# Reordering the first three tiles' layernorm, transposes and loads at the head of a fused attention and feed-forward kernel

## The chip, the cores and the metric

The kernel runs on one core of a Trainium2 chip. A core has TensorE (matrix products and transposes, PE in the profile, its weight loads PEld), VectorE (DVE), ScalarE (ACT), GpSimd (POOL) and SyncE (SP), which here issues every transfer. Each engine takes its own instructions in the order in which they were written; between engines they wait for one another through semaphores. The metric is the device time in microseconds. Three runs of the kernel before took 269.99, 270.53 and 270.79 us: median 270.53.

## The reference

x has 2048 tokens of width 640. It is normalised once, and the result goes through two branches, which are added to x:

```python
x = A_x
xn = _layernorm(x, axis=-1)
return x + _A_ref(xn, A_wqkv, A_w_phi, A_wo) + _B_ref(xn, B_w1, B_w3, B_w2)
```

Branch A is linear attention with 32 heads of width 20. q, k and v are slices of `xn @ wqkv`; q and k are multiplied by a small matrix per head, and phi is the softmax of that product beside the softmax of its negative:

```python
kv = jnp.einsum("bhsf,bhsd->bhfd", phi_k, v)
z  = jnp.einsum("bhsf->bhf", phi_k)
num = jnp.einsum("bhqf,bhfd->bhqd", phi_q, kv)
den = jnp.einsum("bhqf,bhf->bhq", phi_q, z)[..., None] + 1e-6
o = num / den        # heads joined again, then @ wo
```

Branch B is a gated feed-forward layer of width 1536: `(silu(xn @ w1) * (xn @ w3)) @ w2`. Everything comes in and goes out as bf16; products add up in float32.

## The kernel before

The tokens are cut into 16 tiles of 128, the width 640 into 5 chunks of 128. The order of the work is written out by hand (`manual_schedule`, line 127): what stands first in the text stands first on its engine's queue, and no planner moves it. The kernel has three stages: a head in which the tiles are normalised and transposed, V is formed and a few feed-forward products fill in (lines 617 to 702); a loop over tiles for k (706 to 717); and a loop over tiles for q, the attention's output and the result (721 to 751). The branch at line 754 isn't taken for these inputs. The change touches the head, and there tiles 0 to 3 above all.

**The steps of a tile.** `ln_stats` (209) has VectorE take statistics of each half of the tile's width (L213, 320 columns each) and join them (L216); a function given as `between` is called after the first half. `ln_root` (229) takes the square root on ScalarE (L232). `lx` (592) takes the reciprocal on VectorE (L594) and normalises the tile in place, there too (L267). For tiles 0 to 3 `x_transposed`, called `T`, makes five transposes on TensorE (L281) into one PSUM bank, and ScalarE copies them out in two parts, of 256 and of 384 columns (L285); `between` is called after the first. From tile 4 on the root is formed on POOL (`ln_pow`, `ln_newton`) and the transpose is a transfer (L277). `V` (602) runs `by_token` (295): per chunk two products, of 360 and 280 columns, ten in all, with xnT's chunk as the stationary operand and rows of the V weights `wv` as the moving one (L303). `between=(3, f)` calls f ahead of the fourth chunk's products. Three copies by ScalarE follow (L316).

**Loads.** SP's queue begins with x of tiles 0 and 1, three loads of `wv` and x of tiles 2 and 3 (146 to 151). Two more groups are held back: POOL writes one element into the destination from `ry`, the roots, and the load must follow that write. x of tiles 4 to 7 waits in this way for tile 0's root (L619), the first feed-forward weights for tile 1's (L624).

**Warm-up.** `warm(n)` issues n products of zeros on TensorE (L192), 48 ahead of everything and four between the transposes of tiles 0 and 1.

The order at the head, around the change:

```python
ln_stats(1)
ln_root(1)
...
lx(0, 1)
T(0)
warm(4)
lx(1, 1)
T(1)
ln_stats(2)
ln_root(2)
V(0)
```

So on ScalarE the queue is: root of tile 0, root of tile 1, two copies of tile 0, two of tile 1, root of tile 2, the copies of V of tile 0. Then follow tile 3's statistics with tile 2's normalise between the halves, V of tile 1 with tile 2's transposes ahead of its fourth chunk (and tile 3's root between tile 2's two copies), tile 3's normalise, and V of tile 2 with tile 3's transposes.

Of the kernel before, what the change touches and what calls it, by code (L numbers as in the profile page):

```python
# [12 lines left out]
def kernel(  # L13
# [30 lines left out]
    SAFE = 36.0  # L44
    BY_DMA = 4
    BY_ACT = (12, 13)
    WARM = 48


    NCH = 11  # L50
# [65 lines left out]
    def ld(dst, src):  # L116
        nc.sync.dma_start(out=dst, in_=src)
# [9 lines left out]
    with tc.manual_schedule():  # L127
        def ldT(dst, i, d):
            rows = slice(d * P, (d + 1) * P)
            nc.sync.dma_start_transpose(  # L130
                out=dst[:, :, rows], in_=A_wqkv[rows, i * D : (i + 1) * D]
            )
# [3 lines left out]
        def ld_tiles(t, n):  # L136
            ld(
                xin[:, (t // 4) % 3, t % 4 : t % 4 + n],
                x2[t * P : (t + n) * P, :].rearrange("(t p) d -> p t d", p=P),
            )  # L140

        def ld_wv(c, n):
            src = A_wqkv[c * P : (c + n) * P, 2 * D : 3 * D]
            ld(wv[:, c : c + n], src.rearrange("(c p) f -> p c f", p=P))
# [2 lines left out]
        ld_tiles(1, 1)  # L147
        ld_wv(0, 1)
        ld_wv(1, 2)
        ld_tiles(2, 2)  # L150
        ld_wv(3, 2)


        ident = one.tile([P, P], bf, name="ident")
# [35 lines left out]
        def warm(n):  # L190
            for _ in range(n):
                nc.tensor.matmul(idle[:, 0:P], nought[:], nought[:])  # L192

        warm(WARM)

# [13 lines left out]
        def ln_stats(t, between=None):  # L209
            xt = xin[:, (t // 4) % 3, t % 4, :]  # L210
            st = work.tile([P, 2, 6], f32, name="st")
            for i in range(2):
                nc.vector.bn_stats(out=st[:, i, :], in_=xt[:, i * HD : (i + 1) * HD])  # L213
                if i == 0 and between:
                    between()
            nc.vector.bn_aggr(out=mv[:, t, :], in_=st[:])  # L216
# [12 lines left out]
        def ln_root(t):  # L229

            r = slice(t, t + 1)
            nc.scalar.activation(  # L232
                out=ry[:, r], in_=mv[:, t, 1:2], func=AF.Sqrt, bias=eps[:, 0:1], scale=1.0
            )
# [24 lines left out]
        def ln_x(t):  # L259
            xt = xin[:, (t // 4) % 3, t % 4, :]  # L260
            if t in BY_ACT:
                nc.scalar.activation(
                    out=xt, in_=xt, func=AF.Identity,
                    scale=rstd[:, t : t + 1], bias=shift[:, t : t + 1],
                )
                return
            nc.vector.tensor_scalar(  # L267
                out=xt, in0=xt, scalar1=mv[:, t, 0:1], scalar2=rstd[:, t : t + 1],
                op0=ALU.subtract, op1=ALU.mult,
            )  # L270
# [21 lines left out]
        def tile_of(t):  # L292
            return slice(t * P, (t + 1) * P)
# [19 lines left out]
        def v_unit(dst, cols, between=(KD, None)):  # L313
            ps = by_token(cols, wv, "pv", CH, between)
            for p, c0, n, k in chunks(ps):
                nc.scalar.copy(  # L316
                    out=dst[:, c0 : c0 + n, 1 : 1 + k],
                    in_=p.rearrange("p (c e) -> p c e", c=n),
                )
# [272 lines left out]
        def lx(t0, n):  # L592
            if t0 < BY_DMA:
                nc.vector.reciprocal(out=rstd[:, t0 : t0 + n], in_=ry[:, t0 : t0 + n])  # L594
            for t in range(t0, t0 + n):
                ln_x(t)
# [3 lines left out]
        T = x_transposed  # L600

        def V(t, between=(KD, None)):
            v_unit(vaug[:, t], tile_of(t), between)
# [15 lines left out]
        nc.gpsimd.tensor_copy(out=xin[0:1, 1, 0, 0:1], in_=ry[0:1, 0:1])  # L619
        ld_tiles(4, 2)  # L620
        ld_tiles(6, 2)
        ln_stats(1)
        ln_root(1)
        nc.gpsimd.tensor_copy(out=w1[0:1, 0, 0:1], in_=ry[0:1, 1:2])  # L624
        ld_glu(0, 256)
# [1 line left out]
        ld_tiles(10, 2)  # L627
        ld_glu(256, 512)
        ld(wps[:], A_w_phi.rearrange("h j f -> (h j) f").rearrange("(c p) f -> p c f", p=P))
        lx(0, 1)  # L630
        T(0)
        warm(4)
        lx(1, 1)
        T(1)
        ln_stats(2)
        ln_root(2)
        V(0)

        def third():
            T(2, between=lambda: ln_root(3))  # L640
# [3 lines left out]
        lx(3, 1)  # L644
        V(2, between=(3, lambda: T(3)))
        nc.scalar.activation(out=table[:], in_=nought[:, 0:1], func=AF.Tanh)
        ld_tiles(12, 2)
        ld_tiles(14, 2)
        ldT(wkT, 1, 0)
        V(3)  # L650
        stats(4, 2)
# [153 lines left out]
```

## Time and profile before

| what | value |
|---|---|
| median of three runs | 270.53 us (269.99 to 270.79) |
| the profiled execution | 269.93 us |
| its span, first to last instruction | 268.2 us |
| TensorE busy | 262.5 us, 98% of the span |
| VectorE busy | 188.6 us, 70% |
| ScalarE busy | 111.6 us, 42% |
| POOL busy | 95.5 us, 36% |
| granted clock | 1.000 |

A busy TensorE isn't TensorE at its best: its ends are modelled, and products overlap in the records. Of use is where an engine waited and for whom. In a row of a timeline stand the start in us, the time taken, the engine, the line, the operation, output and inputs, the count, and in brackets the idle time before it and what ended that. In the list of waits the three numbers are total us, times, and the longest. In the chain of waits each row is a start, a length and what held the chain there.

### The profile page before, as it was taken

What the parts mean: (1) busy time and instruction counts of PE and PEld (TensorE: products, weight loads), DVE (VectorE), ACT (ScalarE), POOL (GpSimd) and SP (SyncE); (2) the same over time, 40 slices, a digit from 0 to 9 for tenths busy, and PEclk for the clock granted to TensorE, in tenths of its full rate; (3) what the DMA queues carried; (4) which work ended last, traced back from release to release, by engine and by line L of the source; (5) the groups of instructions that cost most, each with busy time, mean ns of one, the idle gap of its engine ahead of it and who ended that gap; (6) DMA issues with size and microseconds to landing.
All of it is one profiled execution on the core that took longest, in us unless ns stands there. A gap on an engine that the chain in (4) does not pass through costs nothing.

```text
span 268.2 us, 5248 instructions
## 1 busy us (share of the span) xinstructions
PE 262.5 (98%) x1973; PEld 166.1 (62%) x1990; DVE 188.6 (70%) x348; ACT 111.6 (42%) x342; POOL 95.5 (36%) x99
## 2 busy tenths in 40 slices
PE   7999999999999999999999999999999999999995
PEld 7646566555555555555555445677777777777773
DVE  4899940887766677777777888966766777776341
ACT  3844568544555554346556545422222222221000
POOL 5055730454433333334444321233344444433000
DMA  6996547970000000000000874355564555566831
GB/s 213 352 223 124 77 99 225 266 195 2 0 0 2 1 2 0 0 4 0 0 2 0 244 160 102 77 132 128 116 149 122 152 127 130 130 146 135 155 98 55
DMA packets 62909, 27.81 MB, mean 104 GB/s; under 512 B 49952, under 2 KB 61600, under 8 KB 62880
## 3 DMA queue, kind: packets, MB, share of 16 engines
q1 hardware_dynamic: 62880, 27.43, 41.9%
q8 instruction: 17, 0.28, 0.4%
q14 instruction: 12, 0.10, 0.1%
HBM read 12.81 MB, written 2.62 MB: 58 GB/s over the span
## 4 chain that ended last, share of the span: by engine, by line
PE 89%; DVE 4%; POOL 2%; issue 1%; ACT 1%; DMA 1%; DVEq 0%
PE acc L525 28%; PE up L401 18%; PE gp L401 17%; PE pq L303 8%; PE pk L303 8%; PE pv L303 5%; DVE st L213 2%; PE pr L462 2%; PE pkv L427 2%; PE pf L385 1%; DMA reg_h<-in_A_x_dram 1%; DVE reg_h L267 1%; POOL ry L227 1%; DVE mv L216 1%; DVE gs L414 0%
## 5 line engine op out<-in xcount | busy, mean ns | idle before, releaser
L367 POOL TENSOR_TENSOR phi<-phi,rk 128x1320 bf16<-128x1320 bf16 x32 | 77.3, 2414 | 134.1 <-DVE rk L366 91.7
L364 DVE TENSOR_REDUCE sk<-phi 128x66 f32<-128x1320 bf16 x32 | 48.9, 1528 | 41.8 <-ACT phi L330 40.8
L401 PEld LDWEIGHTS <-w 128*128 128x128 bf16 x480 | 45.6, 98 | 50.6
L401 PE MATMUL up<-xnT,w 128*128 128x512 bf16 x237 | 59.5, 379 | 0.3
L401 PE MATMUL gp<-xnT,w 128*128 128x512 bf16 x226 | 58.5, 378 | 0.6
L303 PEld LDWEIGHTS <-xnT 128*128 128x128 bf16 x480 | 45.4, 98 | 21.4 <-ACT xnT L285 0.7
L525 PE MATMUL acc<-reg_v,reg_h 128*128 128x320 bf16 (+2 forms) x384 | 54.9, 299 | 0.0
L330 ACT ACTIVATE phi<-pq 128x360 bf16<-128x360 f32 (+2 forms) x96 | 24.8, 364 | 58.0 <-issue 44.1
L525 PEld LDWEIGHTS <-reg_h 128*128 128x128 bf16 x384 | 37.3, 98 | 14.4
L409 ACT ACTIVATE th<-gp 128x512 f32<-128x512 f32 x48 | 28.9, 602 | 32.9 <-PE gp L401 32.4
L417 DVE SCALAR_TENSOR_TENSOR reg_h<-gs,up 128x512 bf16<-128x512 bf16 x48 | 33.0, 688 | 4.9
L330 ACT ACTIVATE phi<-pk 128x360 bf16<-128x360 f32 (+2 forms) x96 | 24.8, 364 | 24.1 <-PE pk L303 24.1
L414 DVE SCALAR_TENSOR_TENSOR gs<-th,gp 128x512 bf16<-128x512 f32 x48 | 31.5, 657 | 0.3 <-ACT th L409 0.3
L534 DVE TENSOR_TENSOR res<-acc,xr 128x320 bf16<-128x320 f32 (+2 forms) x32 | 14.3, 487 | 20.0 <-PE acc L525 20.0
L303 PE MATMUL pk<-wkphi,xnT 128*128 128x360 bf16 (+1 forms) x160 | 24.5, 299 | 0.0
L525 PE MATMUL acc<-reg_w,reg_v 128*128 128x320 bf16 (+2 forms) x160 | 24.5, 299 | 0.0
L303 PE MATMUL pq<-wqphi,xnT 128*128 128x360 bf16 (+1 forms) x160 | 24.3, 299 | 0.0
L303 PE MATMUL pv<-reg_w,xnT 128*128 128x360 bf16 (+1 forms) x160 | 23.6, 299 | 0.2 <-DVE gs L414 0.2
L366 DVE RECIPROCAL rk<-sk 128x66 f32<-128x66 f32 x32 | 18.1, 566 | 3.5 <-DVE sk L364 0.5
L525 PEld LDWEIGHTS <-reg_v 128*128 128x128 bf16 x160 | 15.7, 98 | 6.1
L316 ACT CAST reg_v<-pv 128x360 bf16<-128x360 f32 (+2 forms) x48 | 13.2, 353 | 7.8 <-PE pv L303 7.6
L213 DVE BATCH_NORM_STATS2 st<-reg_h 128x6 f32<-128x320 bf16 x32 | 13.8, 470 | 2.6 <-DMA reg_h<-in_A_x_dram 2.6
(66 smaller groups left out, 132.6 us busy)
## 6 DMA issues: line engine op xcount, KB each, us to landing
w<-in_B_w_dram SPq DMA_DIRECT2D x2, 1280.0 KB, 8.7
xr<-in_A_x_dram SPq DMA_DIRECT2D x16, 160.0 KB, 2.5
out_dram<-res SPq DMA_DIRECT2D x15, 160.0 KB, 1.8
reg_h<-in_A_x_dram SPq DMA_DIRECT2D x7, 320.0 KB, 4.1
reg_v<-in_B_w_dram SPq DMA_DIRECT2D x1, 1920.0 KB, 9.0
w<-in_B_w_dram SPq DMA_DIRECT2D x4, 320.0 KB, 6.4
reg_w<-in_A_wo_dram SPq DMA_DIRECT2D x1, 800.0 KB, 4.7
reg_w<-in_A_wqkv_dram SPq DMA_DIRECT2D x2, 320.0 KB, 4.0
```

The source lines that it names most:

```text
L213: nc.vector.bn_stats(out=st[:, i, :], in_=xt[:, i * HD : (i + 1) * HD])
L303: nc.tensor.matmul(ps[i][:, 0 : b - a], xnT[:, c, cols], w[:, c, a:b], start=(c == 0), stop=(c == KD - 1), skip_group_check=True,)
L330: nc.scalar.activation(out=dst[:, c0 : c0 + n, g, 0:k], in_=p.rearrange("p (c f) -> p c f", c=n), func=AF.Exp, scale=1.0 - 2.0 * g,)
L364: nc.vector.reduce_sum(out=sk[:], in_=rows, axis=AX.X)
L366: nc.vector.reciprocal(out=rk[:], in_=sk[:])
L367: nc.gpsimd.tensor_mul(out=rows, in0=rows, in1=rk[:, :, :, None].to_broadcast([P, 2 * NCH, 3, Dh]))
L401: nc.tensor.matmul(ps[:], w[:, c, fi * P : (fi + 1) * P], xnT[:, c, sc * 512 : (sc + 1) * 512], start=(c == 0), stop=(c == KD - 1),)
L409: nc.scalar.activation(out=th[:], in_=gp[:], func=AF.Tanh, scale=0.5)
L414: nc.vector.scalar_tensor_tensor(out=gs[:], in0=th[:], scalar=1.0, in1=gp[:], op0=ALU.add, op1=ALU.mult)
L417: nc.vector.scalar_tensor_tensor(out=hT[:, 4 * sc : 4 * sc + 4, fi, :], in0=gs[:].rearrange("p (t s) -> p t s", t=4), scalar=0.5, in1=up[: ...
L525: nc.tensor.matmul(ps[:, 0 : b - a], rows[j][0], rows[j][1][:, a:b], start=(j == 0), stop=(j == len(rows) - 1),)
L534: nc.vector.tensor_tensor(out=res[:, a:b], in0=ps[:, 0 : b - a], in1=xr[:, a:b], op=ALU.add)
```

## The change

- `lx(0, 1)`, tile 0's reciprocal and normalise, moves from behind tile 1's statistics to between their two halves.
- `T(1)` moves from ahead of `V(0)` to ahead of V(0)'s fourth chunk, and `ln_root(2)` follows it there; in the text `ln_stats(2)` now stands ahead of both.
- Of the warm-up's 48 products four move to behind `T(0)`.
- x of tile 2 is loaded alone, ahead of the last two row blocks of `wv`, and x of tile 3 behind them; before, one load brought both ahead of these rows.
- x of tiles 12 to 15 comes in one load instead of two.

```diff
-    WARM = 48
+    WARM = 44
...
         ld_wv(1, 2)
-        ld_tiles(2, 2)
+        ld_tiles(2, 1)
         ld_wv(3, 2)
+        ld_tiles(3, 1)
...
-        ln_stats(1)
+        ln_stats(1, between=lambda: lx(0, 1))
         ln_root(1)
...
-        lx(0, 1)
         T(0)
-        warm(4)
+        warm(8)
         lx(1, 1)
-        T(1)
         ln_stats(2)
-        ln_root(2)
-        V(0)
+
+        def second():
+            T(1)
+            ln_root(2)
+
+        V(0, between=(3, second))
...
-        ld_tiles(12, 2)
-        ld_tiles(14, 2)
+        ld_tiles(12, 4)
```

On ScalarE the queue is then: root of tile 0, root of tile 1, two copies of tile 0, two of tile 1, root of tile 2, the copies of V of tile 0: the same order as before. On VectorE tile 0's reciprocal and normalise change places with the second half of tile 1's statistics; the rest keeps its order. On TensorE the transposes of tile 1 stand behind six of V(0)'s ten products, and the eight warm-up products directly ahead of V(0).

## The prediction

> **What bounds the kernel now.** I read the page first, then who TensorE waited for, then the chain of waits through the first 13 us, and last the timeline of each engine there. The profiled execution took 269.93 us, its span 268.2, so 1.73 us lie around the span. The median of the three timed runs, 270.53, is 0.60 above it; I make the sum against the profiled execution and put the difference onto the median. Part 1 of the page, and then TensorE's waits over the whole span:
>
> ```profile
> PE 262.5 (98%) x1973; PEld 166.1 (62%) x1990; DVE 188.6 (70%) x348; ACT 111.6 (42%) x342; POOL 95.5 (36%) x99
> ```
>
> ```profile
> PE idle L192 <- DVE nought L188: 1.1, 1, 1.1
> PE pst L281 <- POOL w L624: 0.4, 1, 0.4
> PE pv L303 <- DVE gs L414: 0.2, 1, 0.2
> ```
>
> TensorE is dense to the end. Its last listed wait is V of tile 7 at 26.32 us, 0.24 us long, on VectorE. Behind it nothing waits, so what the change is worth is how far it shifts the work that reaches that point. That goes back to a chain through the layernorm of tiles 0 to 3; the chain of waits there:
>
> ```profile
> 6.84 2.26 PE pv L303 x16
> 9.10 0.32 PE pst L281 x5
> 9.45 0.37 ACT xnT L285
> 9.82 0.20 ACT ry L232
> 10.02 0.02 issue
> 10.05 0.17 DVE rstd L594
> ...
> 10.61 0.89 DVE st L213 x2
> ```
>
> The reader should see one loop between engines: the transposes of tile 2 (9.10), ScalarE's copy, tile 3's root behind that copy on the same queue, the reciprocal, and VectorE's statistics of tile 4 at 10.61. From 10.61 to 26 us VectorE has a single gap, 0.30 us at 15.01, and that one waits on POOL work which itself waits for those statistics. So a shift of the 10.61 row arrives whole at 26.32. ScalarE's timeline, VectorE's and TensorE's:
>
> ```profile
> 5.30 0.29 ACT L232 ACTIVATE ry<-mv,eps 128x1 f32<-128x1 f32 x1 [0.63 <-DVE rstd L594]
> 6.32 1.41 ACT L285 COPY xnT<-pst 128x256 bf16<-128x256 bf16 x4 [0.73 <-PE pst L281]
> 7.93 0.29 ACT L232 ACTIVATE ry<-mv,eps 128x1 f32<-128x1 f32 x1 [0.19 <-DVE mv L216]
> ...
> 9.72 0.30 ACT L232 ACTIVATE ry<-mv,eps 128x1 f32<-128x1 f32 x1
> 9.91 0.47 ACT L285 COPY xnT<-pst 128x384 bf16<-128x384 bf16 x1
> ```
>
> ```profile
> 5.33 0.45 DVE L267 TENSOR_SCALAR reg_h<-reg_h,mv,rstd 128x640 bf16<-128x640 bf16 x1
> ...
> 6.76 0.89 DVE L213 BATCH_NORM_STATS2 st<-reg_h 128x6 f32<-128x320 bf16 x2 [0.43 <-DMA reg_h<-in_A_x_dram]
> 7.69 0.21 DVE L216 BATCH_NORM_AGGREGATE mv<-st 128x2 f32<-128x12 f32 x1
> ...
> 8.46 0.45 DVE L267 TENSOR_SCALAR reg_h<-reg_h,mv,rstd 128x640 bf16<-128x640 bf16 x1
> ```
>
> ```profile
> 6.75 2.35 PE L303 MATMUL pv<-reg_w,xnT 128*128 128x360 bf16 x16
> 8.96 0.45 PE L281 MATMUL pst<-ident,reg_h 128*128 128x128 bf16 x5
> ```
>
> Today tile 2's root (7.93) starts as soon as its statistics allow; all four copies of tiles 0 and 1 (6.32 to 7.73) are over. VectorE's 0.43 us wait for x of tiles 2 and 3 is what holds it.
>
> **The change, part by part.** Steps between rows, all start to start and from this timeline: statistics pair to aggregate 0.92 (3.14 to 4.06); second half alone to aggregate 0.52 (8.82 to 9.34); aggregate to root 0.24 (7.69 to 7.93); root's end to reciprocal 0.03 (10.02 to 10.05); reciprocal to normalise 0.20; normalise to next statistics 0.36 (8.46 to 8.82); normalise to transposes 0.50 (10.25 to 10.75); transposes to copy 0.49 (8.96 to 9.45); copy to V's first product 0.43 (6.32 to 6.75). On ScalarE the next instruction starts 0.27 after a 256-column copy, 0.36 after a 384-column copy, 0.19 after a root (9.45, 9.72, 9.91, 10.27). One V product is 0.136 (ten in the chain's 1.36 rows), five transposes 0.33.
>
> *Normalising tile 0 between the halves.* Tile 0's root ends at 4.67 as now; the reciprocal follows at 4.70, normalise at 4.90 instead of 5.33, transposes at 5.40 instead of 5.83: 0.43 earlier. But tile 1's second statistics half now waits for that normalise: 5.26, aggregate 5.78 instead of 5.06, root 6.02 instead of 5.30: 0.72 later. Queued behind that root on ScalarE are tile 0's copies. The transposes are ready for them at 5.89, they start at 6.21, against 6.32 now. So of 0.43 us only 0.11 reaches V of tile 0: 6.64 instead of 6.75. The second copy ends at 6.95, before the third pair of products (7.18).
>
> *Warm-up 48 to 44, and 4 to 8.* The first loop's products end 0.055 each earlier (4 in 0.22 of the chain, 6.28), about 5.16 instead of 5.38, before the 5.40 they must clear. The eight run from 5.73 to 6.17 and are hidden by the wait for the copies up to 6.64. Nothing on the path. A bound: at the first loop's slow rate, (4.33 - 0.22) less 19 at 0.055 over 29, about 0.11, eight cost 0.86 and would end at 6.59, still below 6.64.
>
> *Tile 1 transposed inside V of tile 0.* Its root at 6.02 ends at 6.31, reciprocal 6.34, normalise 6.54, ready 7.04. TensorE reaches the transposes after six products, 6.64 + 0.82 = 7.46, where they ran at 6.39 before in a stretch in which TensorE waited for copies anyway. Two costs follow. On TensorE, V of tile 0 and the first six products of tile 1 end at 7.46 + 0.33 + 0.54 + 0.82 = 9.15, against 8.92 now. On ScalarE, tile 1's copies start at 7.95 and 8.22, and **tile 2's root is queued behind them**: 8.58 instead of 7.93. The DVE side was ready: statistics of tile 2 at 6.90 (normalise of tile 1 plus 0.36), aggregate 7.82.
>
> *What is late next.* Root ends 8.87, reciprocal 8.90, normalise of tile 2 at 9.10 (8.46 now), transposes at 9.60 (8.96 now; TensorE idle from 9.15), copy 10.09, tile 3's root 10.36, reciprocal 10.69, normalise 10.89, statistics of tile 4 at 11.25 against 10.61. **Shift: +0.64 us.** Waiting for it: tile 3's transposes (11.39 for 10.75), then the gate and up products, which follow without a gap.
>
> *x of tile 2 alone, x of tile 3 last.* Now both land at 2.67 + 4.1 = 6.77 and V's last weight rows at 3.18 + 4.4 = 7.58. Alone, tile 2 lands no later than 6.77, and 6.90 is when VectorE asks, so the old 0.43 us wait goes but its gain is taken by VectorE's delay. V's last rows move half a load earlier (needed at 7.79). Tile 3 lands about 7.6 to 8.1 (an issue 0.5 later, the same 4.4); VectorE asks at 7.95 and has until 8.46 before the reciprocal of 8.90 slips. Cost 0; the bound above is in the rivals. SP issues one descriptor batch more, 0.47 us from 3.65, before the 4.94 at which it next has work.
>
> *The gate of the feed-forward loads* hangs on tile 1's root through POOL (L624), so those issues go from 5.93 to 6.65 on SP. The first weights landed at 10.93 and are wanted at 13.04 + 0.64; the second pair's columns landed at 16.09 and 17.1 and are wanted at 17.35 and 18.43 plus the shift. Hidden. Tiles 12 to 15 in one load instead of two take one issue of 0.41 from SP; V of tile 4, at 21.67, wants its transposed x, issued at 16.77 with 2.5 to landing. Hidden both ways.
>
> Sum: +0.64 on 269.93 = 270.57 for a profiled execution, on the median 271.17; I say 271.2, 0.24% slower. A measurement of this kernel can't tell less than about 0.3% (0.81 us) from no change: the three runs alone spread over 0.80.
>
> A page's rule bears on the warm-up. In the Trainium skill, "TensorE: Matmul & The Clock Gate", Part 1, the array runs at half rate until about 3.4 us of sustained work fill a window that is not tied to the kernel's start, so the switch point varies by run. Here the matmul rows fall from 314 to 219 ns at about 4.1 us, which agrees with an early switch; with a switch near 7 us, which no run here shows, both heads become bound by TensorE and by that rule I estimate the loss at 0.4 rather than 0.64.
>
> **The rivals.**
> 1. *The shift as summed*, +0.45 to +0.8. For it: queue order on ScalarE and rows of the same instructions.
> 2. *Only TensorE's order costs.* If tile 2's normalise were in time, TensorE's 9.15 against 8.96 remains: +0.19, to 270.7. It would take a ScalarE that gets past tile 1's copies sooner, or a head later than in this execution, hiding part. The 0.60 between profile and median speaks for some of that.
> 3. *x of tile 3 arrives late.* Its statistics' first half stands ahead of tile 2's reciprocal on VectorE; from a landing at 8.46 on each us costs one. The nearest issue-to-landing rows are 4.1 and 4.4; the longest of such loads in the first 20 us is 7.7, from 3.7 a landing at 11.4 and a loss of 0.64 + 2.9. A landing at 9.0 gives +1.2, 271.7. Against it: the queue is nearly empty of issues between 3.65 and 4.94.
> 4. *Faster.* VectorE spends the 0.43 us that it waited for x, now on time, and tile 2's root is not held by the copies: everything 0.43 earlier, less the 0.24 wait at 26.32 that TensorE's own chain sets as the limit unless it too gains; 270.1 to 270.3. It decides if tile 2's root starts before 7.93. Against it: the root's place on ScalarE behind copies of transposes that TensorE reaches at 7.46.
>
> **How the numbers follow.** Chances: rival 1 0.55, rival 2 0.17, rival 3 0.18, rival 4 0.10. Rival 1 straddles the 0.81 line at its upper end: 0.13 of its 0.55 goes to slower by over 0.3%, with all of rival 3 and 0.03 of rival 2 for a spread of medians. Rival 4 as summed is mostly within 0.3%; 0.06 beyond for a gain that grows on the way. So slower 0.34, same 0.60, faster 0.06. The range 270.3 to 271.9 takes rival 2, rival 1 and the near end of rival 3.
>
> **What would show it.** In the changed kernel's timeline: tile 0's transposes near 5.4, its copies near 6.2 behind tile 1's root at about 6.0; V from about 6.6; tile 1's copies at about 7.95 and tile 2's root at about 8.6; statistics of tile 4 near 11.25; V of tile 7 near 26.9. I am wrong if tile 2's root comes before 8.2, if VectorE waits for x of tile 3 after 8.5, if a feed-forward product waits for a weight load, or if TensorE idles anew behind 26 us.

## The result, and the profile after

The changed kernel takes 270.67 us (median of 22 runs, 270.45 to 271.11) against 270.33 us for the kernel before (22 runs, 269.84 to 271.01). The ratio is 1.0014, its 95% interval 1.0008 to 1.0020: a small loss, and clear of noise. The forecast was 271.2 us, 0.24% slower. The profiled execution took 270.67 us with a span of 268.9, where that of the kernel before took 269.93 and 268.2.

The list of TensorE's waits in the changed kernel:

```profile
PE idle L193 <- DVE nought L189: 1.1, 1, 1.1
PE pv L304 <- ACT xnT L286: 0.3, 1, 0.3
PE pst L282 <- DVE reg_h L268: 0.3, 1, 0.3
PE pv L304 <- DVE gs L415: 0.2, 1, 0.2
```

The wait ahead of tile 0's transposes (0.4) has gone, and two have come, one ahead of V of tile 0 for ScalarE's copy of x, one ahead of tile 2's transposes for VectorE's normalise. Then TensorE's timeline (start, length, line, operation, count):

```profile
5.41 0.45 PE L282 MATMUL pst<-ident,reg_h 128*128 128x128 bf16 x5
...
6.64 0.99 PE L304 MATMUL pv<-reg_w,xnT 128*128 128x360 bf16 x6 [0.33 <-ACT xnT L286]
7.46 0.44 PE L282 MATMUL pst<-ident,reg_h 128*128 128x128 bf16 x5
...
9.62 0.45 PE L282 MATMUL pst<-ident,reg_h 128*128 128x128 bf16 x5 [0.26 <-DVE reg_h L268]
...
26.95 1.25 PE L304 MATMUL pv<-reg_w,xnT 128*128 128x280 bf16 x8 [0.23 <-DVE gs L415]
```

The rows of the kernel before to set beside them, where tile 2's transposes stood at 8.96:

```profile
5.83 0.45 PE L281 MATMUL pst<-ident,reg_h 128*128 128x128 bf16 x5 [0.45 <-POOL w L624]
...
26.32 1.37 PE L303 MATMUL pv<-reg_w,xnT 128*128 128x280 bf16 x9 [0.24 <-DVE gs L414]
```

Tile 0's transposes start at 5.41, 0.42 earlier than before, V of tile 0 only 0.11 earlier, and tile 2's transposes 0.66 later. V of tile 7, the last row with a wait, is 0.63 later. ScalarE's timeline shows the place:

```profile
6.03 0.29 ACT L233 ACTIVATE ry<-mv,eps 128x1 f32<-128x1 f32 x1 [1.36 <-DVE mv L217]
6.23 0.73 ACT L286 COPY xnT<-pst 128x256 bf16<-128x256 bf16 x2
7.95 0.75 ACT L286 COPY xnT<-pst 128x256 bf16<-128x256 bf16 x2 [0.98 <-PE pst L282]
8.58 0.31 ACT L233 ACTIVATE ry<-mv,eps 128x1 f32<-128x1 f32 x1
```

Tile 0's copies (6.23) follow tile 1's root (6.03) directly, and tile 2's root (8.58) follows tile 1's copies (7.95) directly: no bracket with a wait, so the engine was busy, while the root's input had been ready. VectorE's timeline says since when:

```profile
6.92 0.88 DVE L214 BATCH_NORM_STATS2 st<-reg_h 128x6 f32<-128x320 bf16 x2
7.83 0.21 DVE L217 BATCH_NORM_AGGREGATE mv<-st 128x2 f32<-128x12 f32 x1
8.05 0.49 DVE L214 BATCH_NORM_STATS2 st<-reg_h 128x6 f32<-128x320 bf16 x1
8.92 0.16 DVE L595 RECIPROCAL rstd<-ry 128x1 f32<-128x1 f32 x1 [0.38 <-ACT ry L233]
9.12 0.45 DVE L268 TENSOR_SCALAR reg_h<-reg_h,mv,rstd 128x640 bf16<-128x640 bf16 x1
...
11.27 0.88 DVE L214 BATCH_NORM_STATS2 st<-reg_h 128x6 f32<-128x320 bf16 x2
```

The aggregate, which is the root's input, ended at 8.04, and the root began at 8.58. VectorE waits 0.38 us for it, and tile 4's statistics come at 11.27 instead of 10.61.

One regularity makes every profile here easy to read. In each of them the execution's own time is the start of V of tile 7 plus 243.60 to 243.76 us (269.93 - 26.32 = 243.61 before, 270.67 - 26.95 = 243.72 after). Nearly all that differs between these kernels, and between executions of one kernel, is settled ahead of that row. The rows name the place more closely. In all 14 profiles VectorE's statistics of tile 4 start 1.63 to 1.66 us behind tile 2's transposes, and V of tile 7 starts 15.67 to 15.71 us behind those statistics. So the start of tile 2's transposes sets the time, as the prediction had it. Two things hold these transposes. Where they start 0.50 us behind tile 2's normalise, the normalise holds them (8.46 and 8.96 before, 9.12 and 9.62 after); where the distance is longer, TensorE was still at the products that stand ahead of them.

But the rise of the median, 0.34, is about half of what the two profiles show (0.63 at V of tile 7, 0.74 in the execution's own time). The fastest runs of the two kernels lie 0.61 apart (269.84 and 270.45), the slowest 0.10 (271.01 and 271.11). So two questions were open: is the queue behind the copies the cause, and why is so little of it in the median?

### The profile page after: what moved, and what is told of

It is laid out like the page before. It is cut to its first block, busy times and chain, and to the rows that moved or that the text cites. A ratio compares the mean times of both kernels' runs of the same rounds, so it can differ in the third digit from the quotient of the medians.

```text
span 268.9 us, 5247 instructions
## 1 busy us (share of the span) xinstructions
PE 262.9 (98%) x1973; PEld 166.0 (62%) x1990; DVE 188.9 (70%) x348; ACT 111.3 (41%) x342; POOL 95.3 (35%) x99
## 4 chain that ended last, share of the span: by engine, by line
PE 89%; DVE 5%; POOL 3%; issue 1%; ACT 1%; POOLq 0%; DVEq 0%
PE acc L526 27%; PE up L402 18%; PE gp L402 17%; PE pq L304 8%; PE pk L304 8%; PE pv L304 5%; DVE st L214 2%; PE pr L463 2%; PE pkv L428 2%; DVE reg_h L268 1%; PE pf L386 1%; POOL ry L228 1%; DVE mv L217 1%; DVE gs L415 0%; ACT ry L233 0%
```

## The experiments

Times are medians, each against the kernel before on the same chip in the same session; V7 is the start of V of tile 7 (of the row behind its wait) in the one profile. In the later sessions the kernel before had medians of 270.42 (rows 3 to 6), 270.34 (rows 7 and 8) and 270.38 (the last three rows).

| kernel | median us (runs) | ratio to before, 95% | V7 us |
|---|---|---|---|
| before | 270.33 (22) | 1 | 26.32 |
| changed | 270.67 (22) | 1.0014 (1.0008 to 1.0020) | 26.95 |
| changed, root between the copies | 270.43 (12) | 0.9997 (0.9988 to 1.0005) | 27.52 |
| before, tile 1 inside V only | 270.81 (12) | 1.0012 (1.0002 to 1.0022) | 27.05 |
| before, tile 0's normalise only | 270.58 (12) | 1.0003 (0.9992 to 1.0013) | 27.05 |
| before, loads only | 270.18 (12) | 0.9992 (0.9983 to 1.0002) | 26.43 |
| before, x of tiles 2 and 3 sooner | 270.28 (11) | 0.9998 (0.9989 to 1.0007) | 26.66 |
| the same, transposes of tiles 2 and 3 sooner | 270.05 (11) | 0.9993 (0.9983 to 1.0002) | 26.18 |
| the same, fewer warm-up products | 270.02 (11) | 0.9987 (0.9978 to 0.9996) | 26.16 |
| before, 24 and 4 warm-up products | 271.54 (5) | 1.0046 (1.0032 to 1.0060) | 27.91 |
| changed, 20 and 8 warm-up products | 271.78 (5) | 1.0045 (1.0031 to 1.0058) | 28.70 |

**Tile 2's root between tile 1's copies.** Theory A says that the root queued behind both copies is the loss, rival B that only TensorE's order costs.

```diff
         def second():
-            T(1)
-            ln_root(2)
+            T(1, between=lambda: ln_root(2))
```

> The changed kernel with one edit: tile 2's root stands between tile 1's two copies on ScalarE, as tile 3's does between tile 2's. Theory A (the loss is the root queued behind both copies): the root starts near 8.2 instead of 8.58, tile 2's normalise near 8.75, its transposes near 9.25, tile 4's statistics near 10.9 instead of 11.27; the profiled span is about 0.35 us under the changed kernel's 268.9 and the median falls by 0.2 to 0.4. Rival B (only TensorE's order costs, the root is hidden): transposes of tile 2 stay near 9.6 and the span within 0.1 of 268.9.

The median is 0.24 us under that of the changed kernel (270.43 for 270.67), and level with the kernel before: 0.9997 against the changed kernel's 1.0014. The fastest run is 270.14 against 270.45. The two intervals do not overlap. This is what A expected of the times, and not B. ScalarE's timeline has the root where A put it:

```profile
7.92 0.37 ACT L286 COPY xnT<-pst 128x256 bf16<-128x256 bf16 x1 [0.98 <-PE pst L282]
8.19 0.30 ACT L233 ACTIVATE ry<-mv,eps 128x1 f32<-128x1 f32 x1
8.39 0.47 ACT L286 COPY xnT<-pst 128x384 bf16<-128x384 bf16 x1
```

The rest of the profile missed, for another reason. VectorE's timeline of the same execution:

```profile
9.07 0.49 DVE L214 BATCH_NORM_STATS2 st<-reg_h 128x6 f32<-128x320 bf16 x1 [1.05 <-DMA reg_h<-in_A_x_dram]
9.48 0.14 DVE L595 RECIPROCAL rstd<-ry 128x1 f32<-128x1 f32 x1
9.66 0.45 DVE L268 TENSOR_SCALAR reg_h<-reg_h,mv,rstd 128x640 bf16<-128x640 bf16 x1
```

x of tile 3, now the last load of its group, landed only at 9.07 in this execution, 5.4 us after its issue. Tile 3's first statistics stand ahead of tile 2's reciprocal on VectorE, so the ready root waited. The execution took 271.24 us, the slowest of the 12, and V7 is 1.20 over that of the kernel before. This is the prediction's rival 3, close to its price (+1.2 for a landing at 9.0), seen once in the five profiles with these loads: in the other four the row starts at 8.05 (the changed kernel), 7.96 (a second profile of it), 8.01 and 8.16. So this profile cannot show the gain of the move; the times do.

It shows something else, in TensorE's timeline:

```profile
1.05 4.81 PE L193 MATMUL idle<-nought 128*128 128x128 bf16 x44 [1.05 <-DVE nought L189]
5.69 0.44 PE L282 MATMUL pst<-ident,reg_h 128*128 128x128 bf16 x5
...
6.62 0.99 PE L304 MATMUL pv<-reg_w,xnT 128*128 128x360 bf16 x6
```

The 44 warm-up products took 4.81 us here instead of 4.29, and tile 0's transposes came 0.28 later than in the changed kernel's profile (5.69 for 5.41). V of tile 0 started no later (6.62 for 6.64), because the copies wait for tile 1's root anyway. The changed order covered this delay whole.

**Tile 1 inside V, alone.**

```diff
-        T(1)
         ln_stats(2)
-        ln_root(2)
-        V(0)
+        def second():
+            T(1)
+            ln_root(2)
+        V(0, between=(3, second))
```

> The kernel before with one part of the change: tile 1's transposes and tile 2's root inside V of tile 0; loads, warm-up and tile 0's normalise as before. Theory A: V of tile 0 at 6.75, tile 1's transposes at 7.57, its copies at 8.06 and 8.33, tile 2's root at 8.69, tile 2's transposes at 9.71 against 8.96: the span 0.75 us over 268.2. Rival B (TensorE's order alone): transposes of tile 2 at 9.26, the span 0.3 over 268.2.

The span is 269.0, 0.8 over 268.2, and tile 2's transposes start at 9.72: A to 0.01, while B had 9.26. VectorE's timeline, then ScalarE's, show one thing more:

```profile
7.09 0.89 DVE L213 BATCH_NORM_STATS2 st<-reg_h 128x6 f32<-128x320 bf16 x2 [0.99 <-DMA reg_h<-in_A_x_dram]
```

```profile
8.04 0.75 ACT L285 COPY xnT<-pst 128x256 bf16<-128x256 bf16 x2 [0.98 <-PE pst L281]
8.68 0.31 ACT L232 ACTIVATE ry<-mv,eps 128x1 f32<-128x1 f32 x1
```

x of tiles 2 and 3 landed at 7.09 here, 0.33 later than in the profile of the kernel before. It cost nothing, because the root was held until 8.68 by the copies anyway. The median rose by 0.39 us only, again about half of what the profile shows.

**Tile 0's normalise between the halves, alone.** The edit is the change's lines for `WARM`, `ln_stats(1, between=...)` and `warm(8)`, with T(1) left ahead of V(0).

> The kernel before with one part of the change: tile 0's normalise between the halves of tile 1's statistics, warm-up 44 and 8; tile 1's transposes stay ahead of V of tile 0. Theory A (ScalarE and VectorE order carry the cost): tile 1's root at 6.03, its normalise at 6.56, tile 1's transposes at 7.06 and so V of tile 0 at about 7.4 instead of 6.75; tile 2's transposes near 9.57, the span 0.6 over 268.2. Rival (normalising tile 0 earlier helps by itself): V of tile 0 near 6.6 and a span under 268.2.

TensorE's timeline, then VectorE's:

```profile
7.01 0.45 PE L281 MATMUL pst<-ident,reg_h 128*128 128x128 bf16 x5 [0.32 <-DVE reg_h L267]
7.30 2.54 PE L303 MATMUL pv<-reg_w,xnT 128*128 128x360 bf16 x16
9.72 0.45 PE L281 MATMUL pst<-ident,reg_h 128*128 128x128 bf16 x5
```

```profile
7.53 0.89 DVE L213 BATCH_NORM_STATS2 st<-reg_h 128x6 f32<-128x320 bf16 x2 [0.57 <-DMA reg_h<-in_A_x_dram]
```

Normalising tile 0 earlier is no help by itself: tile 1's transposes wait to 7.01 and V of tile 0 starts at 7.30, not 6.6. That part is as theory A had it. That tile 2's transposes are at 9.72 instead of 9.57 has a load in it, x of tiles 2 and 3 landing at 7.53 this time: tile 2's normalise starts at 9.22 and the transposes 0.50 behind it. The median is 0.16 us over, and its interval takes in no change; the fastest run is 0.44 over (270.35 against 269.91).

**The loads, alone.** The edit is the change's load lines at the head, and tiles 12 to 15 in one load.

> The kernel before with one part of the change: x of tile 2 alone ahead of V's last weight rows and x of tile 3 behind them, tiles 12 to 15 in one load. Theory A (the order on VectorE decides): tile 2's statistics start at about 6.47 instead of 6.76, but x of tile 3 lands near 8.05 and its first half of statistics stands ahead of tile 2's reciprocal, so tile 2's normalise is near 8.7 instead of 8.46 and the span 0.2 over 268.2. Rival (an earlier tile 2 is a gain, and late x of tiles 2 and 3 is what makes the executions of the kernel before differ): a median 0.2 to 0.4 below 270.33 and a narrower spread of its runs than 1.1.

Each side was half right. VectorE's timeline:

```profile
6.80 0.89 DVE L214 BATCH_NORM_STATS2 st<-reg_h 128x6 f32<-128x320 bf16 x2 [0.50 <-DMA reg_h<-in_A_x_dram]
...
8.01 0.49 DVE L214 BATCH_NORM_STATS2 st<-reg_h 128x6 f32<-128x320 bf16 x1
8.42 0.14 DVE L595 RECIPROCAL rstd<-ry 128x1 f32<-128x1 f32 x1
8.61 0.45 DVE L268 TENSOR_SCALAR reg_h<-reg_h,mv,rstd 128x640 bf16<-128x640 bf16 x1
```

Tile 3's x at 8.01 holds tile 2's normalise to 8.61, as A said (span 268.3). Tile 2's x came no earlier for being alone (6.80; expected 6.47). The median is 0.24 us under the 270.42 of the kernel before in that session, as the rival said (against the 270.33 that it named it is 0.15), and the runs spread over 0.80 us against 1.61 in the same session, though over 12 runs against 35; the interval of the ratio still takes in 1.

**Why the kernel before varies.** The loads' result gave a theory for the missing half: its executions differ because x of tiles 2 and 3 lands at a varying time (M2). The rival is TensorE's clock, which opens at a varying time (M1): by that is meant here the moment at which the rows of products of one size turn from 314 to 219 ns. The granted clock is 1.000 in all three profiles of the kernel before and does not show it. The first of these kernels brings x of tiles 2 and 3 half a load sooner, the second moves the transposes as well; the other two are the kernel before unchanged.

```diff
-        ld_wv(0, 1)
-        ld_wv(1, 2)
+        ld_wv(0, 2)
         ld_tiles(2, 2)
+        ld_wv(2, 1)
         ld_wv(3, 2)
```

> The kernel before with the loads at its head in another order: V's rows of chunks 0 and 1, x of tiles 2 and 3, V's rows of chunk 2, then 3 and 4; nothing else moved. Theory M2 (executions of the kernel before differ because x of tiles 2 and 3 lands at a varying time, 6.8 to 7.5 us, and in most of them holds the head): x lands near 6.3, half a load earlier, tile 2's transposes stay near 8.92 by TensorE's order, so the profiled span is within 0.1 of 268.2, but the median falls by 0.2 to 0.4 against the kernel before and the runs spread over less than 0.8 instead of 1.1 or more. Rival M1 (they differ because the clock of TensorE opens at a varying time): median within 0.1 of the kernel before and the same spread.

> The kernel before once more, one profile. M2: this execution's time above 269.9 follows how far x of tiles 2 and 3 lands behind 6.77, as VectorE's wait at tile 2's statistics shows. M1: it follows when the warm-up products turn from 314 to 219 ns, about 4.1 us in the first profile, and not the landing.

> The kernel before a third time, one profile. The same as for the second: M2 ties the time to the landing of x of tiles 2 and 3, M1 to the moment at which the warm-up products turn from 314 to 219 ns.

The sooner x left the median where it was (270.28 against 270.34), and the spread too (0.93 against 0.66 us): M2 as the main reason is not borne out. In the profile of the sooner x VectorE starts tile 2's statistics at 6.38 without a wait, and yet tile 2's transposes are late, at 9.34, behind warm-up products that were slow to the end, and the execution took 270.38 us. TensorE's timeline in the first profile of the kernel before, then in the second:

```profile
1.05 4.33 PE L192 MATMUL idle<-nought 128*128 128x128 bf16 x48 [1.05 <-DVE nought L188]
```

```profile
1.05 5.30 PE L192 MATMUL idle<-nought 128*128 128x128 bf16 x48 [1.05 <-DVE nought L188]
6.14 0.74 PE L281 MATMUL pst<-ident,reg_h 128*128 128x128 bf16 x5
...
7.36 2.34 PE L303 MATMUL pv<-reg_w,xnT 128*128 128x360 bf16 x16
9.54 0.44 PE L281 MATMUL pst<-ident,reg_h 128*128 128x128 bf16 x5
```

In the second the 48 warm-up products run slow to the end: 5.30 us instead of 4.33, so tile 0's transposes start behind them at 6.14, not 5.83, and run slow too. V of tile 0 is at 7.36 instead of 6.75, tile 2's transposes at 9.54 instead of 8.96. V7 is 26.86, the time 270.46: 0.53 over the first profile. The x of tiles 2 and 3 was early in it (6.51). The third profile took 270.12 us, with an early clock, and TensorE's timeline there has the other reason:

```profile
7.84 1.52 PE L303 MATMUL pv<-reg_w,xnT 128*128 128x360 bf16 x10 [0.32 <-DMA reg_w<-in_A_wqkv_dram]
```

V's last weight rows were late. V7 is 26.52, 0.20 over the first. So both kinds occur; of the three profiles of the kernel before, the one with the late clock lost most.

The Trainium skill, "TensorE: Matmul & The Clock Gate", Part 1, says that the array turns fast after about 3.4 us of work, judged in a window that isn't tied to the kernel's start, so that it varies by run. The profiles agree that it varies by run: products turn from 314 to 219 ns at about 4.1 us in the first profile, near 5.4 with tile 1 alone inside V, and near 7.0 in the second profile of the kernel before. With the first product at 1.05, the first of these is about 3.0 us of work, a little less than the 3.4 stated; the measurement decides.

**A slow clock forced on both.** With `WARM` at 24 for the kernel before and at 20 for the changed one, TensorE idles about 2 us ahead of tile 0's transposes.

> The kernel before with 24 warm-up products instead of 48, to make TensorE slow through the whole head of every execution. If a slow TensorE takes over the head: tile 2's transposes near 11 to 11.7, where TensorE's own products end, the median 1.5 to 2.8 us over the kernel before. The pair with the changed kernel's order decides: see there. If TensorE turns fast by 5.8 all the same, the time is that of the kernel before.

> The changed kernel with 20 and 8 warm-up products, the counterpart of the kernel before with 24 and 4. Theory M1 (a late clock makes both heads TensorE-bound and hides the changed order): V of tile 0 starts earlier, near 6.8 against 7.3, tile 1's transposes cost inside it what they cost ahead of it, and tile 2's transposes come within 0.2 us of the counterpart's; the two medians lie within 0.2 us. Rival (the 0.64 us of the order are paid whatever the clock does): this median 0.45 to 0.7 us above the counterpart's.

> The changed kernel once more, one profile. If its clock opens late (warm-up products at 314 ns to the end), M1 expects V of tile 7 within 0.3 of the kernel before's late execution, 26.86; if it opens near 4.3 as in the first profile, V of tile 7 at 26.95 again.

The first is 1.16 us over the kernel before, less than expected, since its clock opened during V of tile 0. The two ratios are the same, 1.0046 and 1.0045; the medians lie 0.24 us apart, by five runs each, a little over what M1 allowed and well under the rival's 0.45. TensorE's timeline in the changed order:

```profile
8.30 0.74 PE L282 MATMUL pst<-ident,reg_h 128*128 128x128 bf16 x5
8.83 2.68 PE L304 MATMUL pv<-reg_w,xnT 128*128 128x360 bf16 x10
11.35 0.44 PE L282 MATMUL pst<-ident,reg_h 128*128 128x128 bf16 x5
```

Tile 2's transposes start without a wait: tile 2's normalise began at 10.26, 1.09 us ahead of them where 0.50 is enough, and was in time; TensorE's own products held them. With a slow TensorE the root behind the copies is off the path, as M1 has it. The two profiles can't be set against each other beyond that (tile 2's transposes at 10.57 and 11.35, not within 0.2), because the clock opened at different times in them; and intervals of 0.14% each way on five runs don't exclude a gap of some tenths. The changed kernel's second profile took 270.60 us with an early clock and V7 at 26.88, so no profile here shows the changed kernel itself with a late one; the nearest is the version with the root between the copies, whose clock opened near 5.6 and which lost nothing by it at V of tile 0.

**A version that is faster than both.** With x of tiles 2 and 3 sooner, their transposes move ahead of V's third chunk, and then the warm-up shrinks:

```diff
-    WARM = 48
+    WARM = 42
...
-        warm(4)
+        warm(1)
...
-        V(1, between=(3, third))
+        V(1, between=(2, third))
...
-        V(2, between=(3, lambda: T(3)))
+        V(2, between=(2, lambda: T(3)))
```

> As the kernel with x of tiles 2 and 3 half a load sooner, and the transposes of tiles 2 and 3 ahead of the third chunk of V instead of the fourth. If the loop between tile 2's root and tile 4's statistics bounds the head, tile 2's root is at 7.62, its transposes at 8.65 instead of 8.96, tile 4's statistics at 10.3 instead of 10.61: span near 267.9, median 0.4 to 0.6 under the kernel before. If TensorE's own work bounds it instead, tile 4's statistics come earlier but V of tile 7 stays near 26.3: the same time as without the second edit.

> The kernel with x of tiles 2 and 3 half a load sooner and their transposes ahead of V's third chunk, and 42 and 1 warm-up products instead of 48 and 4. If the warm-up itself delays tile 0's transposes in the executions where it stays slow (6.14 instead of 5.83 in the second profile of the kernel before), the slow end of the runs moves down by 0.3 to 0.5 and the median by 0.1 to 0.2 against the version with 48: 0.4 to 0.5 us under the kernel before. If fewer products make the clock open later, the median rises by up to 0.5.

Moving the transposes gave 270.05 against 270.34, 0.29 us, of which the interval does not quite exclude nothing. V7 came at 26.18 although tile 0's transposes were 0.2 late in that profile, and tile 4's statistics at 10.50 instead of 10.61: the loop that ends at these statistics bounds the head, and not the sum of TensorE's products up to V7. Fewer warm-up products brought the slowest run from 271.19 to 270.39 but left the median, 270.02: the expected 0.1 to 0.2 did not come. In its profile tile 2's transposes start 0.66 behind tile 2's normalise, so TensorE's own products hold them there. Together they are 0.36 us under the kernel before, ratio 0.9987 (0.9978 to 0.9996). TensorE's timeline:

```profile
5.75 0.45 PE L281 MATMUL pst<-ident,reg_h 128*128 128x128 bf16 x5 [0.63 <-POOL w L624]
...
8.84 0.44 PE L281 MATMUL pst<-ident,reg_h 128*128 128x128 bf16 x5
...
26.16 1.52 PE L303 MATMUL pv<-reg_w,xnT 128*128 128x360 bf16 x10 [0.20 <-DVE gs L414]
```

## Why the prediction was right, and by how much it was off

- *The path.* Right: the rows of the changed kernel show it, tile 1 alone inside V repeats it (9.72 for 9.71), and the times after moving the root agree. Tile 1's root came at 6.03 (6.02 forecast), V of tile 0 at 6.64 (6.64), tile 1's transposes at 7.46 (7.46), tile 2's root at 8.58 (8.58), its transposes at 9.62 (9.60), tile 4's statistics at 11.27 (11.25), V7 at 26.95 (near 26.9).
- *The gain of 0.43 at tile 0.* Right that 0.11 of it reaches V, the copies being queued behind tile 1's root.
- *Warm-up at no cost.* Right in the changed kernel's profiles. In the kernel before it is not free in every execution, as its second profile shows (6.14 for 5.83). What was wrong in general is that it was read from one profile with an early clock. The prediction's sentence that no run shows a turn near 7 us held only of what had been run by then: the second profile has one, and its execution took 0.53 us longer.
- *The loads at no cost.* The bound was right, the value not always. x of tile 3 was asked for at 7.95 and came at 8.05 in the profile, inside the margin to 8.46; in another kernel with that load order it came at 9.07 and cost over half a microsecond. Rival 3 was seen in one profile of five; nothing shows it in the median.
- *The sum against the median.* This term was mis-sized: +0.64 was put whole on the median, and 0.34 was measured. It holds between the fastest runs, 0.61. Of the 0.53 us between the forecast and the measured time, 0.20 is the median of three runs that it started from (270.53, where 22 runs give 270.33), and the rest is this term, but for the rounding. The profile behind the sum, 269.93 us, was as fast as the second fastest of the 22 runs, so the sum priced the change for one of the best executions of the kernel before; both profiles of the changed kernel (270.67 and 270.60) lie at its median. The kernel before has executions that are later for a late clock (0.53 in one profile) or a late load (0.20 in another), and a held root covers such delays in part: a load 0.33 late cost nothing with tile 1 inside V, and with a slow clock the changed order is off the path. The loads can weigh more than 0.20: in three further profiles with the same loads at the head x of tiles 2 and 3 was first read at 7.09, 7.53 and 7.91, and tile 2's normalise follows that by 1.69 to 1.70 us where no copy holds the root (6.76 and 8.46, 7.53 and 9.22, 7.91 and 9.61). In the kernel before a landing behind 6.76 is then paid in full; in the changed order the root is held until 8.58, and by the 1.17 us from landing to root I estimate that x of tile 2 may land up to 7.4 for nothing. Against it stands the median that the sooner x left where it was. Which share is the clock's and which the loads' was not settled. Rival 2 named this direction, a head later than in the profiled execution.
- *Luck.* The measured 270.67 is the time that rival 2 was given (270.7), and the rise of 0.34 lies between its +0.19 and the +0.45 at which rival 1 began. The times alone would have spoken for rival 2; the rows speak for rival 1. That the time lies inside the range owes something to its width.
- *What a measurement can tell.* The prediction put the least change that can be told from none at 0.3%. It took the spread of three runs for it; 22 runs of each kernel tell 0.14% from nothing.
- *Rival 4, faster.* It decided at a root before 7.93; it came at 8.58.

## What to carry to other kernels

A step moved earlier gains only what the queue in front of its reader lets through: follow the reader's engine in order, and look there for what the moved step itself has pushed back. When a kernel's runs spread by more than the change is worth, one profile prices the change for one kind of execution; take two or three profiles of the kernel before and ask which of its delays the change would cover. An instruction that waits for a load and stands ahead of a ready one on an in-order engine makes the load's worst landing count, not its usual one.

## What was not expected of the hardware

The same loads, issued at the same time, land at varying times: x of tiles 2 and 3, issued together at 2.67, was first read at 6.51, 6.76 and 6.91 in three profiles of one kernel and at 7.09, 7.53 and 7.91 in three kernels with the same loads at the head, and x of tile 3, issued at 3.65, landed 4.5 us later at the most in four profiles and 5.4 us later in the fifth. Splitting x of tiles 2 and 3 did not bring tile 2 forward by half a load: the statistics that waited for it began at 6.80 against 6.76 for both together, one profile each, and a gain smaller than the spread just named would not show. And the moment at which TensorE's products turn from 314 to 219 ns lay between about 4.1 and 7.0 us in the profiles with 42 or more warm-up products, for a first product at 1.05 in every one.
